# An unused buffer in HBM, a 1 KB write to it, and fifteen small loads in the queue of a decode kernel

## The chip, the cores and the metric

The kernel runs on one core of a Trainium2 chip. A core has TensorE (PE; its weight loads are listed apart as PEld), VectorE (DVE), ScalarE (ACT), GpSimd (POOL), SyncE (SP), and 16 DMA engines that carry data between HBM and the core's own memory, SBUF. The metric is the device time of one execution in microseconds (us). The program was run three times for the time; one further execution was taken by the profiler.

## The reference

The reference mixes two blocks that see the same single token x (512 numbers) by a gate g. Block A is attention with 32 query heads over 8 cached heads of keys and values, 32768 positions of 128 numbers each; block B is a SwiGLU feed-forward layer of width 1792.

```
g = sigmoid(sum(x * gate_w))
a: q = x @ wq                       # 32 heads of 128
   scores = q . k_cache / sqrt(128) # 8 cached heads, 4 query heads on each, 32768 positions
   a = (softmax(scores) @ v_cache) @ wo
b = (silu(x @ w_gate) * (x @ w_up)) @ w_down
out = g * a + (1 - g) * b           # 512 numbers
```

All inputs are bf16. The two caches hold 67 MB each; they are nearly all of the 148 MB that are read.

## The kernel before

**Stages.** At the start TensorE computes q, the gate and the hidden row of the feed-forward layer. Then a loop runs over the G = 8 cached heads. For each head the keys are turned with transposes on TensorE (`emit_fill`, L371, into the PSUM tiles pst), copied by VectorE to ktT (L765), multiplied with the queries (`emit_scores`, L383), and their maximum is found; ScalarE takes the exponentials (L633); the values of the head before are multiplied with them (`emit_v`, L440). At the end come the last head's values, the down projection of the feed-forward layer (wd and wx) and the output projection (wo), and two stores write the 512 results.

**Pages.** SBUF holds five pages of 32 KB on each of 128 partitions. One head of K or V is 128 partitions x 64 KB, two pages. Even heads of K lie in the pages B and C, odd ones in A and B; V has the two pages from PG_V on, which q's weights and the gate weights use before. The V of the last head goes to the pages B and C (PG_L).

**The queue of SP.** All large loads are issued by SP in one fixed order, in `load_k` and `load_v` and the lines behind them: q's weights, the two feed-forward weights, K of head 0, then for g = 1 to 7 K of head g and V of head g-1, then V of head 7, then w_down in three parts (L350, L358) and wo in five (L363). A load of K waits until TensorE has turned the first half of the K before (`sem_fill`, L311), a load of V until the V before has been used (`sem_v_free`, L335). SP waits in order: what stands behind a waiting load waits too. From head 2 on a K load is a single transfer of 8.4 MB, as is every V load.

**The other queues.** ScalarE issues the loads of two single rows, x_row and gw_row (L612, L613), then waits for the gate's sum and computes the sigmoid (L615). At the end SP and ScalarE store half of the result each (`emit_store`, L270), two rows of 256 bytes, and SP waits for both (L822).

In the lists of DMA queues, q1 is SP's queue, q10 is ScalarE's, and q8 brings blocks of 16 KB of instructions.

Of the kernel before, what the change touches and what calls it, by code (L numbers as in the profile page):

```python
# [8 lines left out]
BF16 = mybir.dt.bfloat16  # L9
# [3 lines left out]
def bass_gated_mix__gqa_block_cached__swiglu_ffn__decode_kernel(  # L13
# [61 lines left out]
    NPG = 5  # L75
    assert G % 2 == 0
    PAD = 768

    XH, XE, XQ, FX = 2, 4, 4, 4
    XP = XE * XQ  # L80
# [6 lines left out]
    with ExitStack() as es:  # L87
        def S_(name):
            return es.enter_context(nc.semaphore(name))
# [9 lines left out]
        sem_ld_g = S_("s_ld_g")  # L99
        sem_ld_wd = S_("s_ld_wd")  # L100
        sem_ld_wx = S_("s_ld_wx")
        sem_wz = S_("s_wz")
        sem_ones = S_("s_ones")
        sem_dc = S_("s_dc")
        sem_pz = S_("s_pz")
# [42 lines left out]
        def T(name, shape, dt):  # L148
            return es.enter_context(nc.sbuf_tensor(name, shape, dt))

        x_row = T("x_row", [1, D], BF16)
        gw_row = T("gw_row", [1, D], BF16)
# [15 lines left out]
        tX = T("tX", [XS, FX], BF16)  # L168
        pad = T("pad", [128, PAD // 2], BF16)
        page = T("page", [128, NPG, PAGE], BF16)  # L170
# [14 lines left out]
        O2a = T("O2a", [128, WOJ], BF16)  # L185
        O2 = T("O2", [128, WOJ], BF16)
        res_row = T("res_row", [128, 128], BF16)

        def P(name, shape, dt):
            return es.enter_context(nc.psum_tensor(name, shape, dt))  # L190
# [32 lines left out]
        def vrows(pg):  # L223
            return page[:, pg, :].rearrange("p (r d) -> p r d", d=DH)

        wq_v = page[:, PG_Q, 0 : KC * H * DH].rearrange("p (c n) -> p c n", c=KC)
        wgu = page[:, PG_F, 0 : 2 * KC * F].rearrange("p (w c f) -> p w c f", w=2, c=KC)
        wz = page[0:XS, PG_A, 0 : FX * NOUT]
# [40 lines left out]
        def emit_store(eng, half, rows):  # L269
            eng.dma_start(  # L270
                out[0, 0, 256 * half : 256 * (half + 1)].rearrange("(c n) -> c n", c=2),
                rows[31 + 64 * half : 33 + 64 * half, :],
            ).then_inc(sem_out, 16)

        with nc.Block("main") as block:
# [27 lines left out]
            @block.sync  # L303
            def _(sp):
                def load_k(g):
                    lo = PG_A if g % 2 else PG_B
                    dst = page[:, lo : lo + NB, :].rearrange("p b (r d) -> p b r d", d=DH)
                    src = A_k_cache[0, g, :, :].rearrange("(p b r) d -> p b r d", b=NB, r=R)
                    if g > 1:
                        sp.wait_ge(sem_fill, UPG * (g - 1) + UPP)  # L310
                        sp.dma_start(  # L311
                            dst.rearrange("p b r d -> p (b r d)"),
                            src.rearrange("p b r d -> p (b r d)"),
                        ).then_inc(sem_k[0], 16)
                        return
                    for b in range(NB):
                        first = lo + b == PG_B
                        if g and first:
                            sp.wait_ge(sem_fill, UPP)
                        sp.dma_start(dst[:, b, :, :], src[:, b, :, :]).then_inc(  # L320
                            sem_k[0] if first else sem_k1 if g else sem_k[1], 16
                        )

                def load_v(g):
                    src = A_v_cache[0, g, :, :].rearrange("(p b r) d -> p b r d", b=NB, r=R)
                    if g == G - 1:
                        lo, sem = PG_L, sem_vl
                        sp.wait_ge(sem_fill, UPG * g + UPP)
                    else:
                        lo, sem = PG_V, sem_v  # L330
                        if g:
                            sp.wait_ge(sem_v_free, STEP * (g + 1))
                        else:
                            sp.wait_ge(sem_pe_h, 1)
                    sp.dma_start(  # L335
                        page[:, lo : lo + NB, :].rearrange("p b n -> p (b n)"),
                        src.rearrange("p b r d -> p (b r d)"),
                    ).then_inc(sem, 16)

                sp.dma_start(wq_v, A_wq.rearrange("(p c) n -> p c n", c=KC)).then_inc(sem_q, 16)  # L340
                for w, src in enumerate((B_w_gate, B_w_up)):
                    sp.dma_start(
                        wgu[:, w, :, :], src.rearrange("(p c) f -> p c f", c=KC)
                    ).then_inc(sem_f, 16)
                load_k(0)
                for g in range(1, G):
                    load_k(g)
                    load_v(g - 1)
                load_v(G - 1)
                sp.dma_start(  # L350
                    wd[:, :, :], B_w_down[0:FR, :].rearrange("(p j) n -> p j n", j=FM)
                ).then_inc(sem_ld_wd, 16)
                sp.wait_ge(sem_wz, 1)
                rest = B_w_down[FR:F, :].rearrange(
                    "(h q e i) n -> h e q (i n)", h=XH, q=XQ, e=XE
                )
                for h in range(XH):
                    sp.dma_start(wx[h], rest[h]).then_inc(sem_ld_wx, 16)  # L358
                sp.wait_ge(sem_v_free, STEP * G)
                src = A_wo.rearrange("(p j) n -> p j n", j=WOJ)  # L360
                for k, s in enumerate(sem_wo):
                    a, b = WO_CUTS[k], WO_CUTS[k + 1]
                    sp.dma_start(wo_v[:, a:b, :], src[:, a:b, :]).then_inc(s, 16)  # L363
# [246 lines left out]
            @block.scalar  # L610
            def _(act):
                act.dma_start(x_row[0:1, :], A_x[0, :, :]).then_inc(sem_ld_x, 16)  # L612
                act.dma_start(gw_row[0:1, :], gate_w.unsqueeze(0)).then_inc(sem_ld_g, 16)  # L613
                act.wait_ge(sem_pe_g, 1)
                act.activation(  # L615
                    g_col[:, :], ps_m[:, M_G0 : M_G0 + 1], ACT.Sigmoid
                ).then_inc(sem_act_g, 1)
                act.wait_ge(sem_pe_h, 1)
                act.activation(sg, pst[1][:, 0:FS], ACT.Sigmoid).then_inc(sem_act_sg, 1)

                act.wait_ge(sem_ones, 2)
                act.activation(eone[:, :], ones_f[:, 0:1], ACT.Exp).then_inc(sem_exp, STEP)

                with act.Fori(0, G * STEP, STEP) as i:
                    act.wait_ge(sem_v_free, i + STEP)
                    act.activation(part, ps_o[:, :], ACT.Copy).then_inc(sem_acc, STEP)  # L626
                    act.wait_ge(sem_nbias, i + STEP)
                    odd = (i & STEP) * (R // STEP)
                    sc = ps_all[:, :, :].rearrange("p b (t h) -> p h (b t)", h=HPG)
                    for b in range(NB):  # L630
                        bank = R - odd if b else odd
                        for h in range(HPG):
                            act.activation(  # L633
                                ET[:, b * R : (b + 1) * R, h],
                                sc[:, h, bass.ds(bank, R)],
                                ACT.Exp,
                                bias=nbias[:, h : h + 1],
                                scale=SCALE,
                                accum_out=esum[:, b, h : h + 1],
                            ).then_inc(sem_exp, 2)  # L640
                act.wait_ge(sem_v_free, (G + 1) * STEP)
                act.activation(part, ps_o[:, :], ACT.Copy).then_inc(sem_acc, STEP)
# [166 lines left out]
        pe, act, dve, sp = nc.tensor, nc.scalar, nc.vector, nc.sync  # L809
# [9 lines left out]
        for half, eng in enumerate((sp, act)):  # L819
            eng.wait_ge(sem_dve_row, 1)  # L820
            emit_store(eng, half, res_row)
        sp.wait_ge(sem_out, 32)  # L822


# [26 lines left out]
```

## Time and profile before

| | us |
|---|---|
| time, median of 3 runs (lowest to highest) | 349.12 (348.97 to 349.30) |
| the profiled execution | 349.16 |
| its span, first to last instruction | 347.8 |
| TensorE matmuls busy | 260.8 (75%) |
| VectorE busy | 186.6 (54%) |
| ScalarE busy | 33.4 (10%) |
| packets of SP's queue, share of 16 DMA engines | 98.7% |
| read from HBM | 148.11 MB, 426 GB/s over the span |

The page lists busy times first, then 40 equal slices of the span with a digit for the busy share of each engine, the DMA queues, the chain of work that ended last, and the costliest groups of instructions. In a DMA queue's line stand packets, MB and the share of 16 engines' time that the packets took, so that a share times 16 times the window's length is the engines' own time.

### The profile page before, as it was taken

How to read it: one execution, taken by the hardware profiler on the slowest of the kernel's cores; microseconds unless marked ns; L12 is line 12 of the kernel's file. 1: busy time of each engine (PE TensorE's matmuls, PEld its weight loads, DVE VectorE, ACT ScalarE, POOL GpSimd, SP SyncE). 2: the span in 40 equal slices, each digit the busy share in tenths (PEclk: the TensorE clock that was granted, in tenths of full speed). 3: DMA queues.
4: the chain of work that ended last, by engine and by line, in shares of the span. 5: the costliest groups of instructions: out<-in, count | busy, mean ns of one | idle time of the engine just before them, and what ended most of it. 6: DMA issues, size and time to landing. Idle time of an engine off the chain costs nothing.

```text
span 347.8 us, 8869 instructions
## 1 busy us (share of the span) xinstructions
PE 260.8 (75%) x3925; PEld 220.6 (63%) x3925; DVE 186.6 (54%) x232; ACT 33.4 (10%) x143; POOL 4.6 (1%) x16
## 2 busy tenths in 40 slices
PE   1354995999749982999459982999469972999475
PEld 1124994998449941997259942996269842996232
DVE  3144995698119931697129921895149820895101
ACT  1002000300130003000300003000400012000400
POOL 3000000000000000000000000000000000002000
PEclk9996999699659987699959985898869985898669
DMA  8999999999999999999999999999999999999996
GB/s 322 419 459 426 420 422 458 469 414 437 414 430 475 415 437 415 437 467 415 437 407 445 467 414 437 407 452 460 414 437 407 452 460 415 437 407 452 406 418 261
DMA packets 3946, 148.21 MB, mean 426 GB/s; under 512 B 450, under 2 KB 580, under 8 KB 868
## 3 DMA queue, kind: packets, MB, share of 16 engines
q1 hardware_dynamic: 3932, 148.11, 98.7%
q8 instruction: 6, 0.10, 0.1%
q10 hardware_dynamic: 8, 0.00, 0.0%
HBM read 148.11 MB, written 0.00 MB: 426 GB/s over the span
## 4 chain that ended last, share of the span: by engine, by line
DMA 64%; PE 33%; DVE 2%; issue 1%; SPq 1%; ACT 0%; DVEq 0%
DMA page<-in_A_k_cache_dram 52%; PE pst L371 24%; DMA page<-in_B_w_up_dram 6%; DMA page<-in_A_wo_dram 6%; PE ps_sc L383 5%; PE ps_o L440 2%; PE pst L535 1%; DVE ktT L722 1%; DVE ktT L765 0%; SPq L363 0%; PE ps_m L553 0%; PE ps_m L566 0%; DVE ktT L712 0%; DVE ktT L710 0%; PE ps_sc L246 0%
## 5 line engine op out<-in xcount | busy, mean ns | idle before, releaser
L765 DVE COPY ktT<-pst 128x2048 bf16<-128x2048 bf16 x128 | 153.3, 1221 | 64.6 <-PE pst L371 60.4
L371 PE MATMUL pst<-ident_f,page 128*128 128x128 f32 x1024 | 147.2, 299 | 39.5 <-DMA page<-in_A_k_cache_dram 38.2
L371 PEld LDWEIGHTS pst<-ident_f,page 128*128 128x128 f32 x1024 | 126.0, 154 | 43.9 <-DMA page<-in_A_k_cache_dram 38.8
L383 PE MATMUL ps_sc<-qcur,ktT 128*128 128x8 bf16 x2048 | 64.1, 166 | 6.3 <-DVE ktT L765 6.3
L383 PEld LDWEIGHTS ps_sc<-qcur,ktT 128*128 128x128 bf16 x2048 | 63.8, 97 | 8.0 <-DVE ktT L765 7.1
L440 PE MATMUL ps_o<-page,ET 128*16 128x512 bf16 x512 | 39.4, 477 | 5.5 <-DMA page<-in_A_v_cache_dram 5.5
L440 PEld LDWEIGHTS ps_o<-page,ET 128*16 128x16 bf16 x512 | 15.0, 107 | 26.1 <-issue 18.8
L633 ACT ACTIVATE ET<-ps_sc,nbias 128x128 bf16 x64 | 23.9, 555 | 49.9 <-DVE nbias L791 49.9
L626 ACT ACTIVATE acc<-ps_o 128x512 f32<-128x512 f32 x8 | 4.8, 597 | 223.8 <-PE ps_o L440 218.9
L783 DVE TENSOR_REDUCE gm<-ps_m 4x1 f32<-4x128 f32 x8 | 2.2, 279 | 40.6 <-PE ps_m L420 40.6
L633 ACT ACTIVATION_READ_ACCUMULATOR ET<-ps_sc,nbias 128x1 f32 x64 | 18.3, 285 | 0.0
L773 DVE TENSOR_REDUCE pmaxf<-ps_sc 128x4 f32<-128x512 f32 x16 | 11.0, 686 | 8.4 <-PE ps_sc L383 8.4
L497 PE MATMUL pst<-page,xT 128*1 128x512 bf16 x32 | 3.6, 627 | 8.9 <-DMA page<-in_A_wq_dram 8.9
L461 PE MATMUL ps_m<-sel,acc 128*128 128x4 f32 x64 | 8.4, 255 | 1.8 <-ACT acc L626 1.6
L461 PEld LDWEIGHTS ps_m<-sel,acc 128*128 128x128 f32 x64 | 7.7, 191 | 2.5 <-ACT acc L626 2.2
L424 PE MATMUL ps_m<-diag,ones_f 4*128 4x4 f32 x16 | 3.8, 306 | 6.8 <-DVE diag L787 6.8
L424 PEld LDWEIGHTS ps_m<-diag,ones_f 4*128 4x128 f32 x16 | 3.3, 259 | 8.4 <-issue 8.4
L750 DVE RECIPROCAL rS<-ps_m 128x4 f32<-128x4 f32 x9 | 1.6, 182 | 12.2 <-PE ps_m L461 12.2
L497 PEld LDWEIGHTS pst<-page,xT 128*1 128x1 bf16 x32 | 0.9, 115 | 10.7 <-issue 10.7
L685 DVE CAST ktT<-pst 128x1024 bf16<-128x1024 f32 x2 | 2.4, 1220 | 8.2 <-PE pst L497 8.2
L452 PEld LDWEIGHTS ps_m<-esum,ones_f 128*128 128x128 f32 x32 | 4.2, 190 | 3.5 <-issue 3.5
L301 POOL MEMSET page<- 48x2048 bf16 x1 | 1.8, 1798 | 311.7 <-PE pst L371 311.7
(76 smaller groups left out, 54.6 us busy)
## 6 DMA issues: line engine op xcount, KB each, us to landing
page<-in_A_k_cache_dram SPq DMA_DIRECT2D x4, 4096.0 KB, 34.9
page<-in_A_wq_dram SPq DMA_DIRECT2D x1, 4096.0 KB, 13.4
page<-in_A_wo_dram SPq DMA_DIRECT2D x1, 2048.0 KB, 17.4
page<-in_B_w_gate_dram SPq DMA_DIRECT2D x1, 1792.0 KB, 17.2
page<-in_B_w_up_dram SPq DMA_DIRECT2D x1, 1792.0 KB, 21.0
wd<-in_B_w_down_dram SPq DMA_DIRECT2D x1, 1664.0 KB, 30.3
page<-in_A_wo_dram SPq DMA_DIRECT2D x1, 1152.0 KB, 19.8
page<-in_A_wo_dram SPq DMA_DIRECT2D x1, 512.0 KB, 20.6
```

The lines of the kernel that those rows point to most:

```text
L371: ins = pe.transpose(pst[u % NST][:, k * 128 : (k + 1) * 128], kv[:, n * 128 : (n + 1) * 128], ident_f[:, :],)
L383: ins = pe.matmul(ps_sc[b][:, col : col + 2 * HPG], kt[:, k, e, :], qcur[:, e, :], start=(e == 0), stop=(e == 1),)
L424: pe.matmul(ps_m[:, M_B0 : M_B0 + HPG], ones_f[0:HPG, :], diag[:, :], start=True, stop=True,).then_inc(sem_b, STEP)
L440: ins = pe.matmul(ps_o[32 * c : 32 * c + RQ * HPG, :], ET[:, n : n + RQ, :].rearrange("p n h -> p (n h)"), v[:, k * RQ : (k + 1) * RQ, :], ...
L452: pe.matmul(ps_m[:, M_S0 : M_S0 + HPG], ones_f[:, :], esum[:, b, :], start=(b == 0), stop=(b == NB - 1),)
L461: ins = pe.matmul(ps_m[:, M_P0 : M_P0 + HPG], acc[:, q, :], sel4[:, q * HPG : (q + 1) * HPG], start=(q == 0), stop=(q == RQ - 1),)
L497: ins = pe.matmul(pst[0][32 * k : 32 * k + 1, t * QN : (t + 1) * QN], xT[:, c : c + 1], wq_v[:, c, n : n + QN], start=(c == 0), stop=(c == ...
L535: ins = pe.matmul(pst[1][32 * k : 32 * k + 1, w * 512 : w * 512 + FS], xT[:, c : c + 1], wgu[:, w, c, k * FS : (k + 1) * FS], start=(c == ...
L626: act.activation(part, ps_o[:, :], ACT.Copy).then_inc(sem_acc, STEP)
L633: act.activation(ET[:, b * R : (b + 1) * R, h], sc[:, h, bass.ds(bank, R)], ACT.Exp, bias=nbias[:, h : h + 1], scale=SCALE, accum_out=esum ...
L765: dve.tensor_copy(ktT[:, n % NKT, :], pst[n % NST][:, :].bitcast(BF16)).then_inc(sem_cp, 1)
L773: dve.tensor_reduce(pmaxf[:, b, :], sc, AX.X, ALU.max).then_inc(sem_d, 1)
```

## The change

Three things are added; nothing is removed.

1. A buffer `spare` of 48 x 1024 bf16 numbers (96 KB) in HBM. ScalarE waits until gw_row has been loaded and then issues a write of that row, 1 KB, to the first row of the buffer. Nothing reads the buffer.
2. A tile `mark` in SBUF, 16 partitions x 15 x 64 numbers, and fifteen loads into it: the first has 15 rows, the next 14, the last 1, each row 64 numbers (128 bytes) from the head of a row of wq. SP issues one behind each load of K from head 1 on and one behind each load of V. Nobody reads the tile.
3. One semaphore counts these loads and the write; SP waits for it at the very end, after it has issued its half of the output and ahead of its wait for the output.

```diff
+    MARKS = list(range(15, 0, -1))
...
+        sem_mark = S_("s_mark")
...
+        mark = T("mark", [16, len(MARKS), 64], BF16)
...
+        spare = nc.dram_tensor("spare", [48, 1024], BF16, kind="Internal").ap()
...
+                marks = list(enumerate(MARKS))
+
+                def load_mark():
+                    if marks:
+                        m, n = marks.pop(0)
+                        sp.dma_start(mark[0:n, m, :], A_wq[0:n, 0:64]).then_inc(sem_mark, 16)
+
...
                 load_k(0)
                 for g in range(1, G):
                     load_k(g)
+                    load_mark()
                     load_v(g - 1)
+                    load_mark()
                 load_v(G - 1)
+                load_mark()
+                assert not marks
...
                 act.dma_start(gw_row[0:1, :], gate_w.unsqueeze(0)).then_inc(sem_ld_g, 16)
+                act.wait_ge(sem_ld_g, 16)
+                act.dma_start(spare[0:1, 0:512], gw_row[0:1, :]).then_inc(sem_mark, 16)
                 act.wait_ge(sem_pe_g, 1)
...
             emit_store(eng, half, res_row)
+        sp.wait_ge(sem_mark, 16 * (len(MARKS) + 1))
         sp.wait_ge(sem_out, 32)
```

## The prediction

> **What bounds the kernel now.** I read the page from its second part downwards: first what is busy all the time, then the chain of waits, then the stages.
>
> ```profile
> span 347.8 us, 8869 instructions
> PE 260.8 (75%) x3925; PEld 220.6 (63%) x3925; DVE 186.6 (54%) x232; ACT 33.4 (10%) x143; POOL 4.6 (1%) x16
> ...
> DMA  8999999999999999999999999999999999999996
> ...
> q1 hardware_dynamic: 3932, 148.11, 98.7%
> q8 instruction: 6, 0.10, 0.1%
> q10 hardware_dynamic: 8, 0.00, 0.0%
> HBM read 148.11 MB, written 0.00 MB: 426 GB/s over the span
> ...
> DMA 64%; PE 33%; DVE 2%; issue 1%; SPq 1%; ACT 0%; DVEq 0%
> ```
>
> TensorE works 75% of the span, the 16 DMA engines 98.7% of it on SP's queue (q1) alone. The chain of waits gives TensorE 33%, and that share needs care: it is there because a K load is released by a transposing TensorE. Whether that costs anything is seen in the stages, in the table of windows (columns: stretch, its length, busy time of PE, PEld, DVE, ACT and POOL, granted clock, DMA share, GB/s):
>
> ```profile
> 0.00:10.00 10.00, 1.31 (x8) 1.16 (x8) 4.29 (x11) 1.28 (x1) 2.80 (x15) 1.00 0.86 339
> 10.00:20.00 10.00, 4.10 (x34) 1.45 (x34) 2.08 (x2) 0.17 (x1) 0.00 (x0) 1.00 0.98 419
> ...
> 100.00:293.00 193.00, 151.33 (x2315) 132.19 (x2315) 108.26 (x125) 17.95 (x85) 0.00 (x0) 0.84 1.00 434
> ...
> 344.00:344.50 0.50, 0.38 (x28) 0.20 (x16) 0.00 (x0) 0.00 (x0) 0.00 (x0) 1.00 0.61 240
> 344.50:345.00 0.50, 0.07 (x7) 0.07 (x10) 0.00 (x0) 0.00 (x0) 0.00 (x0) 1.00 0.66 248
> 345.00:345.50 0.50, 0.33 (x16) 0.16 (x16) 0.00 (x0) 0.00 (x0) 0.00 (x0) 1.00 0.35 121
> 345.50:345.90 0.40, 0.29 (x8) 0.12 (x8) 0.00 (x0) 0.00 (x0) 0.00 (x0) 1.00 0.00 0
> ```
>
> From 100 to 293 us every engine is busy all the time (share 1.00) and the core takes 434 GB/s, 27.1 GB/s for each of 16 engines. No transfer waits there for a released page: the bytes are the bound. At that rate 148.11 MB are 341.3 us. The last four rows show that the engines do not stop together: between 344.0 and 345.5 us the share falls from 0.61 to 0.35 to nothing, so some engines are done about 1.5 us before the last. The kernel ends with the **last** engine: what is added to that one lengthens the span, what is added to an early one is free up to some 1.5 us.
>
> **The change part by part.** The fifteen loads ("marks") of 15, 14, ... 1 rows of 128 B go on SP's queue: 15+14+...+1 = 120 rows, each with its completion write. Nobody reads them. What can they cost: time of DMA engines, time of SP, and the wait at the end.
>
> *DMA engines.* The price of short packets, from the DMA view of three short windows: 345.4 to 345.7, 345.5 to 345.56, and 346.4 to 347.8 us.
>
> ```profile
> DMA packets 9, 0.01 MB, mean 17 GB/s; under 512 B 4, under 2 KB 9, under 8 KB 9
> q1 hardware_dynamic: 9, 0.01, 5.5%
> ...
> DMA packets 2, 0.00 MB, mean 0 GB/s; under 512 B 2, under 2 KB 2, under 8 KB 2
> q1 hardware_dynamic: 2, 0.00, 1.9%
> ...
> DMA packets 8, 0.00 MB, mean 1 GB/s; under 512 B 8, under 2 KB 8, under 8 KB 8
> q1 hardware_dynamic: 4, 0.00, 0.2%
> q10 hardware_dynamic: 4, 0.00, 0.2%
> ```
>
> The second window holds nothing but two completion writes: 1.9% of 16 x 0.06 us is 18 ns, so 9 ns each. The first has five rows of 1 KB (the last of A_wo) and four completions: 5.5% of 16 x 0.3 us is 264 ns, less 36, so 46 ns a row. In the third, each queue stores two rows of 256 B, with two completions: 0.2% of 16 x 1.4 us is 45 ns, less 18, so some 13 ns a row (a rounded share). A row of 128 B is shown nowhere. Bounds: 9 ns (a 4-byte packet) and 46 ns (1 KB); I take 13 ns, the nearest row in size. An engine's own time can only grow with its list, so below nothing is excluded here. So a mark costs an engine that carries one row 13 + 9 = 22 ns, between 18 and 55.
>
> Who carries them? The two-row store left two rows and two completions on its queue, hence one row for each of two engines. By that a mark of n rows loads n engines with one row each; if it is always the first n, one engine gets 15 marks, the next 14, and one none: 15 x 22 = 0.33 us at most (0.27 to 0.83 between the bounds), 7.5 x 22 = 0.165 us on average. The trace doesn't number the engines, so which is the last one is open; I take the average, +0.165 us, with 0 and 0.83 us as the ends.
>
> The Trainium skill (DMA: Bandwidth & Descriptors, "Why a DMA increments its semaphore by 16 and not by 1") says that a DMA from SP or ACT uses the largest count up to 16 that divides the slowest dimension, on the lowest-numbered engines; the four packets of the two-row store agree with the count, and no row shows the numbers. If the loads took turns over all engines instead, each would have 7 or 8 marks and the sum would be the same 0.165 us without a choice.
>
> *SP's queue.* Marks stand between the big loads in SP's program, so V loads are issued behind a mark, and K loads too. From the timeline of SP and the chain in order of time:
>
> ```profile
> 91.53 0.33 SPq L335 DMA_DIRECT2D page<-in_A_v_cache_dram  x1
> 111.69 0.33 SPq L311 DMA_DIRECT2D page<-in_A_k_cache_dram  x1
> 129.78 0.33 SPq L335 DMA_DIRECT2D page<-in_A_v_cache_dram  x1
> ...
> 111.69 27.19 DMA page<-in_A_k_cache_dram
> ...
> 323.45 0.34 SPq L363
> ```
>
> A K load issued at 111.69 lands 27.19 us later. Its own 8.39 MB take 19.3 us at 434 GB/s, so the V load ahead of it had 7.9 us to go. The V load at 129.78 finds the K load with 138.88 - 129.78 = 9.1 us to go. Take off up to 1.5 us by which early engines run ahead: the queue has 6 us of work whenever SP issues. An issue is 0.33 us here, 0.43 at most by the rows of A_wo; a mark before a big load delays it by that much, against 6 us. Cost nothing; if that cover were gone, 15 x 0.4 = 6 us. A mark is also queued between loads on each engine, which is the 22 ns already counted. The A_wo loads at 323.45 wait for the last freed V page and not for a mark.
>
> *ScalarE.* Its new wait for gw_row stands ahead of the 1 KB write and of the sigmoid. From the timeline of ACT and the view of the tile gw_row:
>
> ```profile
> 1.56 1.28 ACT L615 ACT_TABLE_LOAD   x1 [1.56 <-PEq L836]
> 18.41 0.17 ACT L615 ACTIVATE g_col<-ps_m 128x1 f32<-128x1 f32 x1 [15.57 <-PE ps_m L507]
> ...
> L678 DVE TENSOR_TENSOR gp_row<-x_row,gw_row x1: 681/681/681, 8.4 to 8.4; 1x512 f32<-1x512 bf16 x1
> ```
>
> gw_row is in at 8.4 us (its first reader starts there). The issue takes some 0.3 us, the table load, if it slips behind the wait, 1.28 us: ScalarE is ready at 10.0 us for an activation that starts at 18.41. Nothing, with 8 us of cover. The write itself puts one 1 KB row and one completion, 46 + 9 = 55 ns, on one engine.
>
> *The buffer* of 96 KB moves no bytes but the 1 KB. It may shift where other arrays lie; no row prices that, so it is a rival below and nothing in the sum.
>
> *The end.* SP's wait for all marks stands behind the issue of the output:
>
> ```profile
> SPq L822 <- DMA out_dram<-res_row: 1.0, 1, 1.0
> ```
>
> SP waits 1.0 us there for the output anyway; the last mark was in the queue ahead of B_w_down and has long landed. Nothing.
>
> *Sum:* 349.16 us (the profiled execution: 347.8 of span and 1.36 around it; the median of the runs is 349.12, 0.04 below) + 0.165 = **349.3 us**; with the bounds on the price alone 349.1 to 350.0. That is +0.05%; I count up to 0.2% (0.7 us) as no change, about what a measurement of this kernel can tell.
>
> **The rivals.**
>
> *A short row is dear (slower).* The blocks of instructions are the nearest foreign packets: 0.1% of 16 x 347.8 us for six is 0.93 us each (a rounded share), while 16 KB at 27.1 GB/s are 0.60: 0.33 us of stall per interruption. If a mark stops each of its engines like that, an average engine loses 7.5 x 0.33 = 2.5 us, giving 351.7; an engine with all fifteen 5 us, 354. It decides from 0.7 / 7.5 = 93 ns per mark. Against it: completions of 9 ns in the same queue leave the share at 1.00. For it: marks read HBM for 128 B. The Trainium skill (same page, "Specifications") says that below 512 B a transfer needs a read-modify-write, and gives no price; the 256 B stores at 13 ns show none, though they write HBM and not SBUF. 0.19.
>
> *One more block of instructions.* SP gets 15 issues more. If its program crosses into another block, one engine pays 0.93 us: 350.1 if it is a late engine, nothing if an early one. 0.11, of which 0.09 slower.
>
> *Marks hold up SP.* Issues of a few odd rows might take far longer than 0.43 us; they would need 6 us to starve the queue, then about 3 us for the kernel, 352. 0.03.
>
> *All rows of a mark on one engine* (the change doesn't spread as its row counts suggest): 120 x 13 + 15 x 9 = 1.70 us on one engine, 350.9 if it is the last, little if it is early. The two-row store speaks against it. 0.04, of which 0.03 slower.
>
> *Something shifts for the better (faster).* The buffer moves arrays in HBM, or marks bring the engines out of step, and stretches below full rate improve: 10 to 20 us at 419 GB/s, and the uneven end. The first 10 us move 3.39 MB, 7.8 us at full rate, so 2.2 us pass at the start; all there is to win after them is 345.5 - 2.2 = 343.3 against 341.3 for the bytes: 2.0 us, 347.2; half of it 348.2. Against it: the marks come after 44 us and only add work, and 434 GB/s leave nothing in the middle. 0.16.
>
> **How the numbers follow.** The forecast has 0.47. Faster is the last rival, 0.16. Slower: 0.19 + 0.09 + 0.03 + 0.03 = 0.34. Within 0.2%: 0.47 + 0.02 + 0.01 = 0.50. The range reaches down to the middle of the faster case, 348.2 (0.07 left out), and up to 351.5, just short of the middle of the dear-row case (0.11 left out). The forecast's own range is 349.0 to 350.0.
>
> **What the profile of the changed kernel would show.** Right: SP's queue with 240 packets more (4172) and q10 with two more; the stretch of 100 to 293 us still at share 1.00 and 434 GB/s; a K load still landing some 27 us after its issue; the last landing of A_wo later by no more than 0.3 us. A dear row shows as a fall below 434 GB/s in that stretch at a share of 1.00, or a share below 1.00; a further block as q8 with seven packets; a held-up SP as an issue longer than 1 us for the mark; a gain as a higher rate ahead of 44 us or a steeper end after 344. The prediction is wrong if the number of the last engine, or the price of 128 B in the middle of a full queue, is far from the average and the 13 ns taken here.

## The result and the profile after

The changed kernel takes 349.78 us (median of 13 runs, 349.60 to 350.08) against 349.20 (348.97 to 349.33): a ratio of 1.0018, 95% interval 1.0010 to 1.0026. That is 0.6 us more, just inside the 0.2% that the prediction counts as no change, though its interval does not reach 1. The profiled execution took 349.84 us with a span of 348.5. All ratios here are of the executions within 1.5% of a kernel's fastest, which leaves some out only for the two kernels with rows of 512 B further down.

Parts 1 to 4 of the page of the changed kernel:

```profile
span 348.5 us, 8885 instructions
...
q1 hardware_dynamic: 4172, 148.13, 98.6%
q8 instruction: 6, 0.10, 0.1%
q10 hardware_dynamic: 10, 0.00, 0.0%
...
DMA 59%; PE 35%; DVE 3%; issue 2%; SPq 1%; ACT 0%; DVEq 0%
```

The queues hold what was foreseen: 240 packets more on q1, two more on q10, six blocks of instructions as before.

SP's and ScalarE's timelines (start, length, instruction), and the tile view of `mark` (durations in ns: least, median, most):

```profile
111.47 0.33 SPq L315 DMA_DIRECT2D page<-in_A_k_cache_dram  x1
111.83 0.39 SPq L349 DMA_DIRECT2D mark<-in_A_wq_dram  x1
129.48 0.33 SPq L339 DMA_DIRECT2D page<-in_A_v_cache_dram  x1
129.85 0.37 SPq L349 DMA_DIRECT2D mark<-in_A_wq_dram  x1
```

```profile
7.96 0.23 ACTq L630 DMA_DIRECT2D spare<-gw_row  x1
8.22 1.28 ACT L632 ACT_TABLE_LOAD   x1 [8.22 <-DMA gw_row<-in_gate_w_dram]
18.50 0.17 ACT L632 ACTIVATE g_col<-ps_m 128x1 f32<-128x1 f32 x1 [9.00 <-PE ps_m L522]
```

```profile
L349 SPq DMA_DIRECT2D mark<-in_A_wq_dram x15: 289/342/485, 45.6 to 305.8; - x15
```

No mark held SP longer than 0.49 us, and the big loads are issued at the same moments as before (111.47 and 129.48 for 111.69 and 129.78). ScalarE has its table at 9.5 us and waits nine more for TensorE. So the time went neither there nor there.

It went into the DMA engines. The chain in order of time, K loads and the last load of wo (issue, time to landing), before:

```profile
73.44 26.84 DMA page<-in_A_k_cache_dram
...
151.10 26.42 DMA page<-in_A_k_cache_dram
189.38 26.77 DMA page<-in_A_k_cache_dram
227.56 27.23 DMA page<-in_A_k_cache_dram
265.82 27.61 DMA page<-in_A_k_cache_dram
...
324.78 20.75 DMA page<-in_A_wo_dram
```

and after:

```profile
73.92 26.18 DMA page<-in_A_k_cache_dram
111.47 27.43 DMA page<-in_A_k_cache_dram
150.94 26.86 DMA page<-in_A_k_cache_dram
189.33 27.38 DMA page<-in_A_k_cache_dram
227.80 27.59 DMA page<-in_A_k_cache_dram
267.37 26.65 DMA page<-in_A_k_cache_dram
...
324.89 21.21 DMA page<-in_A_wo_dram
```

Add issue and time to get the landings. Before: 100.28, 138.88, 177.52, 216.15, 254.79, 293.43, that is 38.60 to 38.64 apart. After: 100.10, 138.90, 177.80, 216.71, 255.39, 294.02, that is 38.80, 38.90, 38.91, 38.68, 38.63 apart. Five periods take 193.92 us instead of 193.15: 0.77 us were lost, nearly all of it between 100 and 216 us, against 0.18 us gained ahead of them. The last load of wo lands at 346.10, before at 345.53: the 0.6 us of the result. (The chain's rows name the last loads that TensorE waited for.)

### The profile page after: what moved, and what is told of

Same layout as the page of the kernel before. It is cut to its first block, busy times and chain, and to the rows that moved or that the text cites. A ratio compares the mean times of both kernels' runs of the same rounds, so it can differ in the third digit from the quotient of the medians.

```text
span 348.5 us, 8885 instructions
## 1 busy us (share of the span) xinstructions
PE 260.0 (75%) x3925; PEld 219.8 (63%) x3925; DVE 186.6 (54%) x232; ACT 33.4 (10%) x143; POOL 4.6 (1%) x16
## 4 chain that ended last, share of the span: by engine, by line
DMA 59%; PE 35%; DVE 3%; issue 2%; SPq 1%; ACT 0%; DVEq 0%
DMA page<-in_A_k_cache_dram 47%; PE pst L386 25%; DMA page<-in_A_wo_dram 6%; DMA page<-in_B_w_up_dram 6%; PE ps_sc L398 6%; DVE ktT L782 2%; PE ps_o L455 2%; PE pst L550 1%; DVE ktT L739 1%; SPq L378 0%; PE ps_m L568 0%; PE ps_m L581 0%; DVE pmaxf L790 0%; DVE ktT L729 0%; PE ps_sc L250 0%
## 5 line engine op out<-in xcount | busy, mean ns | idle before, releaser
L455 PE MATMUL ps_o<-page,ET 128*16 128x512 bf16 x512 | 38.7, 470 | 6.1 <-DMA page<-in_A_v_cache_dram 6.1
```

The source lines that it names most:

```text
L455: ins = pe.matmul(ps_o[32 * c : 32 * c + RQ * HPG, :], ET[:, n : n + RQ, :].rearrange("p n h -> p (n h)"), v[:, k * RQ : (k + 1) * RQ, :], ...
```

## The experiments

The first question was which part costs the 0.6 us, and how. A mark itself is as cheap as predicted; in a window of 0.021 us of the changed kernel (78.974 to 78.995 us) lie a load's completion, a mark's row and its completion:

```profile
DMA packets 3, 0.00 MB, mean 6 GB/s; under 512 B 3, under 2 KB 3, under 8 KB 3
q1 hardware_dynamic: 3, 0.00, 9.2%
```

9.2% of 16 x 0.021 us is 31 ns: 9 + 13 + 9. My theory was "in step": the falling row counts shift the engines against each other, and engines that come into step slow each other's 64 KB rows. The rivals: "own traffic" (the short rows themselves disturb the big ones), and "place" (the buffer moves arrays in HBM).

**The marks without the buffer, and the buffer without the marks.** Two runs.

```diff
-        spare = nc.dram_tensor("spare", [48, 1024], BF16, kind="Internal").ap()
-                act.wait_ge(sem_ld_g, 16)
-                act.dma_start(spare[0:1, 0:512], gw_row[0:1, :]).then_inc(sem_mark, 16)
...
-        sp.wait_ge(sem_mark, 16 * (len(MARKS) + 1))
+        sp.wait_ge(sem_mark, 16 * (len(MARKS)))
```

> The fifteen loads of 15 to 1 rows without the buffer and without ScalarE's write. Measured for the whole change: 0.6 us over before (349.8 against 349.2), of which some 0.15 us is the marks' own time on the engine that ends last (ten marks of 15 ns). Theory 'in step' (the marks shift the engines against each other by 15 ns steps, and engines that come into step slow each other's 64 KB rows) and theory 'own traffic' (the marks' short rows themselves disturb the big rows): all of it stays, 349.7 to 349.9, and the landings of K between 100 and 216 us are again 38.7 to 38.9 us apart instead of 38.64. Theory 'place' (the buffer moves arrays in HBM): only the marks' own time stays, 349.3 to 349.4, and the landings are 38.66 us apart.

```diff
-    MARKS = list(range(15, 0, -1))
+    MARKS = []
...
-        mark = T("mark", [16, len(MARKS), 64], BF16)
+        mark = T("mark", [16, 15, 64], BF16)
```

> The buffer of 96 KB and ScalarE's 1 KB write without any of the fifteen loads. Theories 'in step' and 'own traffic': as before, 349.1 to 349.3, K landings 38.64 us apart. Theory 'place': 349.6 or more, K landings 38.7 to 38.9 us apart between 100 and 216 us.

The marks alone: 349.84 us, ratio 1.0023 (1.0014 to 1.0032). The buffer and the write alone: 349.33, ratio 1.0002 (0.9994 to 1.0011). "Place" falls; the whole effect is the marks'. With the buffer alone the five periods of K take 193.15 us, as before. In the profile of the marks alone, taken of their fastest run (349.51), K lands 38.64 to 38.76 us apart, where 38.7 to 38.9 was expected between 100 and 216 us: the five periods take 193.40 us, 0.25 more than before. The last load of wo lands at 346.19 all the same, so in that execution most of the time was lost behind the last K.

**Marks of 16 rows, and marks of 1 to 15 rows.** From here on there is no buffer and no write.

```diff
-    MARKS = list(range(15, 0, -1))
+    MARKS = [16] * 15
```

> Fifteen loads of 16 rows each, no buffer and no write: 240 rows instead of 120, but the same on every engine, so that no engine shifts against another. Every engine carries fifteen marks of 15 ns, 0.22 us. Theory 'in step': that and no more, 349.4 to 349.5, K landings 38.67 us apart throughout (two marks of 15 ns in each period). Theory 'own traffic': twice the rows, twice the disturbance, 350.2 to 350.6, K landings 38.9 to 39.1 us apart.

```diff
-    MARKS = list(range(15, 0, -1))
+    MARKS = list(range(1, 16))
```

> The same fifteen loads in rising order, 1 to 15 rows, no buffer and no write. Theory 'own traffic': as with the falling order, 349.7 to 349.9, with the disturbance growing to the end (K landings furthest apart after 216 us). Theory 'in step': the total shift is the same, 14 engines against each other by 15 ns steps, but it comes late; some 349.4 to 349.9, with K landings 38.7 us or more apart only where neighbours meet, not in proportion to the rows. Theory 'place': 349.3 to 349.4.

Even marks: 350.31 us, ratio 1.0027 (1.0017 to 1.0037), where "in step" allowed 349.5 at most. My theory fell: marks that are the same on every engine cost more, not less. Rising marks: 349.60 us, ratio 1.0012 (1.0003 to 1.0021). That is below the 349.7 to 349.9 that "own traffic" gave; against the falling marks the intervals overlap. So "own traffic" as I had put it isn't right either, and the chain of the even marks shows no steady toll:

```profile
44.39 17.07 DMA page<-in_A_k_cache_dram
73.55 27.00 DMA page<-in_A_k_cache_dram
112.07 27.69 DMA page<-in_A_k_cache_dram
151.95 26.46 DMA page<-in_A_k_cache_dram
190.25 26.97 DMA page<-in_A_k_cache_dram
228.63 27.22 DMA page<-in_A_k_cache_dram
268.03 26.52 DMA page<-in_A_k_cache_dram
```

The landings at 61.46, 100.55, 139.76, 178.41, 217.22, 255.85 and 294.55 are 39.09, 39.21, 38.65, 38.81, 38.63 and 38.70 apart, with two marks of sixteen rows in each period from the second on. What such a stall is, a window of 2.5 us around one boundary shows: 98.0 to 100.5 us of the even marks, where 16 engines start a 64 KB row each behind a mark:

```profile
DMA packets 64, 1.05 MB, mean 420 GB/s; under 512 B 48, under 2 KB 48, under 8 KB 48
q1 hardware_dynamic: 64, 1.05, 105.2%
```

and before at the same boundary (97.6 to 100.1 us):

```profile
DMA packets 32, 1.05 MB, mean 419 GB/s; under 512 B 16, under 2 KB 16, under 8 KB 16
q1 hardware_dynamic: 32, 1.05, 97.1%
```

Before: 97.1% of 16 x 2.5 us is 38.84 us; less 16 completions of 9 ns, 38.70 us for 16 rows, 2.42 us each. With marks: 105.2% is 42.08 us; less 16 rows of 13 ns and 32 completions, 41.58, or 2.60 us each. (A share over 100% comes of packets that end behind the window.) So the mark's own packets stay short, and the **next** 64 KB row takes 0.18 us more, on average over the 16 engines. The changed kernel shows it more weakly, here from 137.3 to 139.7 us:

```profile
DMA packets 30, 1.05 MB, mean 437 GB/s; under 512 B 14, under 2 KB 14, under 8 KB 14
q1 hardware_dynamic: 30, 1.05, 102.4%
```

102.4% of 16 x 2.4 us is 39.32 us, less some 0.14 for 14 short packets: 2.45 us a row.

**What in a mark disturbs the next row?** Its read from HBM, its write to SBUF, or its short length. Four runs, all on the even marks. In the third the tile has ten places, used again from the eleventh mark on; in the fourth it spans all 128 partitions.

```diff
-                        sp.dma_start(mark[0:n, m, :], A_wq[0:n, 0:64]).then_inc(sem_mark, 16)
+                        sp.dma_start(mark[0:n, m, :], A_wq[0, 0:1024].rearrange("(r c) -> r c", c=64)[0:n, :]).then_inc(sem_mark, 16)
```

> Fifteen marks of 16 rows as in the run with even marks (350.3; before 349.2), but the sixteen rows of 128 B are one stretch of 2 KB in HBM instead of sixteen places 8 KB apart. The profile of the even marks shows what costs: where a mark lies between two loads, the first 64 KB rows of the next load took up to 281 ns more than 2418 on all engines, at some marks and not at others. Theory 'sixteen reads at a pitch of 8 KB meet in HBM': the stall is gone or falls to a third, 349.4 to 349.7. Theory 'writes meet in SBUF' and theory 'short rows are rewritten': unchanged, 350.1 to 350.5.

```diff
+                pool.memset(msrc[:, :], 1.0).then_inc(sem_msrc, 1)
...
-                        sp.dma_start(mark[0:n, m, :], A_wq[0:n, 0:64]).then_inc(sem_mark, 16)
+                        if m == 0:
+                            sp.wait_ge(sem_msrc, 1)
+                        sp.dma_start(mark[0:n, m, :], msrc[0:n, :]).then_inc(sem_mark, 16)
```

> The same, but the rows come from a small tile in SBUF that GpSimd fills at the start: no read of HBM at all. Theories of HBM reads (at a pitch or in general): 349.4 to 349.6, the fifteen marks' own 0.22 us. Theories of the write (SBUF partitions, rows under 512 B): unchanged, 350.1 to 350.5.

```diff
-                        sp.dma_start(mark[0:n, m, :], A_wq[0:n, 0:64]).then_inc(sem_mark, 16)
+                        sp.dma_start(mark[0:n, m % 10, :], A_wq[0:n, 0:256]).then_inc(sem_mark, 16)
```

> The same marks of 16 rows from HBM at the pitch of 8 KB, with rows of 512 B instead of 128 B (the tile's slots are used again after ten marks). Own time by the line through rows of 128 B (13 ns) and 1 KB (46 ns): 27 ns a row, so 15 x 29 = 0.44 us. Theory 'short rows are rewritten' (a row under 512 B costs a read and a write): the stall is gone, 349.6 to 349.7. Theories of HBM reads and of SBUF partitions: the stall stays or grows, 350.3 to 350.8.

```diff
-                        sp.dma_start(mark[0:n, m, :], A_wq[0:n, 0:64]).then_inc(sem_mark, 16)
+                        sp.dma_start(mark[0:128:8, m, :], A_wq[0:n, 0:64]).then_inc(sem_mark, 16)
```

> The same marks of 16 rows of 128 B from HBM at the pitch of 8 KB, written to the partitions 0, 8, ... 120 instead of 0 to 15. Theory 'writes meet in SBUF' (sixteen engines write sixteen neighbouring partitions, which few of them write otherwise): the stall falls by half or more, 349.4 to 349.9. Theories of HBM reads and of rows under 512 B: unchanged, 350.1 to 350.5.

One stretch of HBM: 349.53 us, ratio 1.0011 (1.0002 to 1.0019), with the same 4412 packets on q1 as the even marks. Source in SBUF: 349.41, ratio 1.0005 (0.9997 to 1.0014). Spread partitions: 350.25, ratio 1.0028 (1.0018 to 1.0038), unchanged. So the disturbance comes with the read of HBM, and of separate places 8 KB apart; where the rows are written does not matter. The same boundary with the source in SBUF (97.6 to 100.1 us) has the same 64 packets and no stall:

```profile
DMA packets 64, 1.05 MB, mean 420 GB/s; under 512 B 48, under 2 KB 48, under 8 KB 48
q1 hardware_dynamic: 64, 1.05, 98.0%
```

98.0% is 39.20 us, less 0.50: 38.70, again 2.42 us a row. Its K landings of 100.18 and 293.47 come from these rows:

```profile
75.77 24.41 DMA page<-in_A_k_cache_dram
...
266.88 26.59 DMA page<-in_A_k_cache_dram
```

They are 193.29 us apart, 0.14 more than before, with ten marks between them: a mark without a stall costs the last engine 14 ns. The run with one stretch of HBM has 193.29 us there too.

Rows of 512 B gave what no theory had: 370.79 us (median of all six runs, 363.9 to 376.6), ratio 1.0465 (1.0428 to 1.0503). I come back to it below.

**The change itself with one stretch of HBM; a pitch of 1 KB; marks late; rows of 512 B in one stretch.** The first of these is the changed kernel with its buffer and its write, and with the first of the four edits above in `load_mark`.

> The whole change (buffer, write, fifteen loads of 15 to 1 rows) with one thing altered: the rows of a mark are one stretch in HBM (128 B apart) instead of 8 KB apart. Theory 'reads at the pitch of 8 KB meet in HBM': the stalls go and the marks' own time stays, 10 to 15 marks of 15 ns at most, 349.3 to 349.45 (before 349.2, the change 349.8). Against it (stalls from the falling row counts, from the order of the engines or from the buffer): 349.7 to 349.9.

349.37 us, ratio 1.0007 (0.9998 to 1.0015), where the change gives 1.0018. With the rows in one stretch the stalls are gone (the five periods of K take 193.14 us), and what is left, 0.13 us with an interval that reaches zero, fits the marks' own time.

```diff
-                        sp.dma_start(mark[0:n, m, :], A_wq[0:n, 0:64]).then_inc(sem_mark, 16)
+                        sp.dma_start(mark[0:n, m, :], A_wo[0:n, 0:64]).then_inc(sem_mark, 16)
```

> Fifteen marks of 16 rows of 128 B at a pitch of 1 KB (rows of wo instead of wq). Measured so far: pitch 128 B 349.5, pitch 8 KB 350.3, before 349.2, own time 0.22. If the pitch counts by degrees: 349.6 to 349.9. If only the largest pitch makes the reads meet: 349.4 to 349.55. If any separate rows do it, whatever the pitch: 350.1 to 350.5.

349.53 us, ratio 1.0010 (1.0002 to 1.0019): a pitch of 1 KB is as harmless as one of 128 B. The run changes the array along with the pitch, so it alone doesn't say which of the two it is; with the run of one stretch, which stayed in wq, the distance of the rows is the better account.

```diff
-    MARKS = [16] * 15
+    MARKS = [0] * 8 + [16] * 7
...
                         m, n = marks.pop(0)
+                        if not n:
+                            return
...
-        sp.wait_ge(sem_mark, 16 * (len(MARKS) + 1))
+        sp.wait_ge(sem_mark, 16 * 7)
```

> Marks of 16 rows of 128 B at the pitch of 8 KB, at the last seven of the fifteen places alone. With all fifteen the stalls lay at the places 2 to 9 and none behind. Theory 'place' (what is loaded next at the places 2 to 9 meets the marks' reads): no stalls here, only 7 x 15 ns, 349.25 to 349.35. Theory 'arrangement' (the first marks after an undisturbed stretch stall until the engines have moved into an order that no longer meets): the stalls come back at these places, 349.8 to 350.3.

349.85 us, ratio 1.0018 (1.0009 to 1.0026), for seven marks. At the boundary of 252.5 to 255 us the profile has

```profile
DMA packets 64, 1.05 MB, mean 420 GB/s; under 512 B 48, under 2 KB 48, under 8 KB 48
q1 hardware_dynamic: 64, 1.05, 99.7%
```

that is 39.88 us less 0.50, 2.46 us a row instead of 2.42. The landings of K at 216.30, 255.07 and 293.86 are 38.77 and 38.79 apart, where the even marks had 38.63 and 38.70. So the stalls come back at places that had none when marks lay ahead of them, and they do not belong to what is loaded there. That the stalls last until the engines have moved into another order is the theory that foresaw this; neither that order nor what in it helps was shown, and seven marks were too few for the stalls to end.

```diff
-                        sp.dma_start(mark[0:n, m % 10, :], A_wq[0:n, 0:256]).then_inc(sem_mark, 16)
+                        sp.dma_start(mark[0:n, m % 10, :], A_wq[0, 0:4096].rearrange("(r c) -> r c", c=256)[0:n, :]).then_inc(sem_mark, 16)
```

> The fifteen marks of 16 rows of 512 B that took 370.8, with the sixteen rows in one stretch of 8 KB of HBM. If the collapse to some 357 GB/s in that run came of the rows' pitch: 349.6 to 349.8 (own time 15 x 29 ns = 0.44 us), the rate 433 to 434 GB/s to the end. If it came of the length of the rows or of the second use of the tile's slots: 360 or more again.

392.4 us (median of all seven runs, 383.4 to 402.6), ratio 1.1011 (1.0985 to 1.1038). So the collapse with rows of 512 B is not the pitch's doing, unlike the stalls.

## Why the prediction was right, and where it fell short

The time lay in the range (349.78 in 348.2 to 351.5, and in the forecast's own 349.0 to 350.0), on the likeliest side. By its steps:

- **The bound.** Right: with all engines busy at 434 GB/s, whatever was added to SP's queue came out at the end, and nothing else did.
- **The price of a 128 B row.** 13 ns predicted from the 256 B stores, 13 ns measured. The sum of 22 ns a mark was somewhat high: in the stream it is 14 ns. Packets overlap a little there (in the kernel before their times add up to 100.2% from 100 to 293 us), which may be why. That 13 and 13 meet is luck in part: the stores' share of 0.2% was rounded, and a shorter window of the kernel before (347.2 to 347.4 us, two rows and two completions on each queue) gives 17 and 15 ns for their rows:

```profile
q1 hardware_dynamic: 4, 0.00, 1.6%
q10 hardware_dynamic: 4, 0.00, 1.5%
```

- **Who carries the marks.** The average of 0.165 us stands beside 0.13 us measured once the stalls are taken out (349.37 against 349.24 in the same session, an interval that reaches zero). The packet counts agree with one row for each of n engines; the profile does not number the engines.
- **SP's queue, ScalarE, the end.** Nothing, as said: issues of 0.29 to 0.49 us, the sigmoid at 18.50 for 18.41, and SP's last wait unchanged:

```profile
SPq L840 <- DMA out_dram<-res_row: 1.0, 1, 1.0
```

- **The buffer.** Nothing, as in the sum: ratio 1.0002 by itself.
- **The step that fell short** is the price of a mark on the DMA engines, taken as "13 + 9 = 22 ns, between 18 and 55": it bounds the mark's own packets and leaves out what the mark does to the 64 KB rows behind it. The measured total is 0.6 us where the sum had 0.165. Some 0.1 us is the marks' own time, and the rest, by the run with rows in one stretch, the stalls of the following rows. The sum's upper end, 350.0, held by luck: the bound of 46 ns a row was wide enough for a cost that it does not name.
- **The rival of the dear short row** had the right ingredient ("marks read HBM for 128 B") and the wrong form. Its stall is per mark and engine, 0.33 us, and would have given 351.7; the real one is 0.18 us on the average next row where the even marks showed it most clearly, depends on how far apart the rows lie in HBM, and in that run was gone behind 217 us, after some eight marks. The argument against it, that completions of 9 ns leave the rate untouched, could not speak to reads.
- **The sign to look for**, "the last landing of A_wo later by no more than 0.3 us", was wrong: 0.57 us. And "434 GB/s leave nothing in the middle" hides the loss, since the stretch of 100 to 293 us still averages 434 GB/s after; the landings of K, to 0.01 us, show it.

The Trainium skill (DMA: Bandwidth & Descriptors, "Specifications") has a read-modify-write for transfers below 512 B. No run here bears out a toll of that kind: rows of 128 B took 13 ns and from SBUF cost nothing that the runs could tell (ratio 1.0005), while rows of 512 B were far worse. The Trainium skill (DMA: Bandwidth & Descriptors, "Latency and other measured facts") lists copies that lose rate when rows lie at large powers of two apart; the runs agree in direction at a much smaller distance, 8 KB costing stalls and 1 KB and 128 B costing none.

## What to carry to other kernels

When the DMA engines are the bound, price a small transfer by two terms: its own packets, and what it does to the rows behind it. The second is read from a window of one row's length, share times 16 engines divided by the rows in it, here 2.60 against 2.42 us. Short rows beside a full stream, here of 128 B, are best taken from SBUF or from one stretch of HBM; one stretch did not help rows of 512 B (next section). A loss of this size shows in the landings of equal loads before it shows in any average rate.

## What was not expected of the hardware

Rows of 512 B in the same marks, 120 KB in all, cost 22 and 43 us by the medians. The windows of the run with rows in one stretch (columns as in the prediction; the profiled execution is the slowest, 402.58 us):

```profile
61.00:100.00 39.00, 31.22 (x466) 26.49 (x465) 22.62 (x30) 6.58 (x33) 0.00 (x0) 0.85 1.01 434
100.00:138.60 38.60, 30.37 (x463) 25.98 (x463) 21.62 (x25) 3.59 (x17) 0.00 (x0) 0.85 1.00 370
138.60:177.20 38.60, 29.64 (x463) 26.55 (x463) 21.20 (x22) 0.60 (x1) 0.00 (x0) 0.84 1.00 354
254.40:293.00 38.60, 20.00 (x312) 17.20 (x309) 13.11 (x19) 3.59 (x17) 0.00 (x0) 0.73 1.01 355
```

and those of the run at the pitch of 8 KB (profiled execution 371.49 us):

```profile
177.20:215.80 38.60, 31.50 (x463) 27.20 (x463) 21.72 (x25) 3.59 (x17) 0.00 (x0) 0.81 1.00 433
215.80:254.40 38.60, 30.69 (x463) 26.46 (x463) 21.62 (x25) 3.59 (x17) 0.00 (x0) 0.85 1.01 408
254.40:293.00 38.60, 29.02 (x463) 25.76 (x463) 21.62 (x25) 3.20 (x16) 0.00 (x0) 0.85 1.00 357
```

The engines stay busy (share 1.00), but the rate falls from 434 to some 355 GB/s and stays there, between marks too, from about 100 us in one run and about 235 us in the other. The fall comes in steps, at marks. Here are two stretches of the first run, between its third and fourth mark and behind the fourth, and one of the other run, behind its tenth:

```profile
101.00:119.00 18.00, 17.93 (x270) 17.34 (x269) 15.73 (x14) 0.00 (x0) 0.00 (x0) 0.93 0.98 379
122.00:142.00 20.00, 8.68 (x133) 4.89 (x129) 3.25 (x10) 3.59 (x17) 0.00 (x0) 0.72 1.02 360
237.00:254.00 17.00, 10.69 (x158) 6.96 (x156) 4.78 (x11) 3.59 (x17) 0.00 (x0) 0.83 0.99 374
```

16 rows of 64 KB are 1.049 MB, so share times 1.049 MB over the rate is the time of a row: 2.71, 2.97 and 2.78 us, against 2.4 us up to 100 us (first row of the first run). In the first run the fall comes long before the tile's slots are used a second time (from the eleventh mark, behind the K load of head 6), so that is not the cause. The kernel before, run in turn with these, stayed between 348.99 and 349.47 us. The Trainium skill (HBM Reference, "Specifications (TRN2)") gives some 358 GB/s as one core's share of its HBM; no run here shows what the other core of that HBM did, and whether the likeness means anything is open. So is the cause: against the marks of 128 B from one stretch what differs is the length of the rows, and with it the bytes read and the size of the tile; why that tips the stream into a lower rate is not shown.
